# Moving one small weight transfer to the head of the load queue in a decode kernel

## The chip, the cores and the metric

The kernel runs on one core of one Trainium2 chip. The metric is device time in microseconds (us) of the whole kernel; the median of several runs is compared.

## What is computed

Two blocks share one normalised input, and their results are added to the input. Block A is attention of one new token per batch row over a cache of 4096 keys and values (4 batch rows, 32 heads, head width 128); block B is a gated MLP with a layer norm on one half of its hidden vector. All inputs are bf16.

```python
xn = layernorm(x)                                   # x: (4, 1, 640)
q  = (xn @ wq) as (B, H, 1, 128)                    # wq: (640, 4096)
p  = softmax(q . k_cache * 128**-0.5)               # k_cache: (4, 32, 4096, 128)
A  = (p . v_cache) @ wo                             # v_cache alike, wo: (4096, 640)
z  = gelu(xn @ w_in)                                # w_in: (640, 1728)
z1, z2 = z[..., :864], layernorm(z[..., 864:])
B  = (z1 * (w_sp * z2 + b_sp)) @ w_out              # w_out: (864, 640)
return x + A + B
```

The two caches are 268 MB of the 282 MB that the kernel reads.

## The kernel before

**Stages.** The kernel first normalises x, computes q for all heads (L287) and block B (L309 to L367), and then streams the caches in units of one batch row and eight heads, 8 MB each: 16 units of K and 16 of V. A K unit is transposed by DVE in eight pieces (L389), each followed by matmuls that give scores (L400). After four K units of one group of heads comes the softmax of that group (L407 to L465), and the four V units follow (L474), interleaved with K units of the next group. At the end the attention output is multiplied with wo (L517), added up (L565 to L580) and stored in two halves (L583).

**Buffers.** One buffer `kv` of five slots holds everything that is loaded in bulk: first the weights wq (slots 0 and 1), w_in and the first 512 rows of w_out (slot 2), then the cache units and wo. A unit takes two half slots or slots, and may be loaded once the work on what lay there is done.

**The remaining 352 rows of w_out.** They do not fill 128 partitions and are loaded by four transfers into two tiles `w_rest` (L128), which are taken from the pool of the transposed keys, `kT`. The table `RB` gives each transfer's partition block, first column, number of groups and columns:

```python
RB = ((0, 0, 8, 7), (0, 7, 5, 1), (1, 0, 3, 7), (1, 7, 3, 2))
```

The first of them moves 224 rows, 280 KB, in 32 pieces of 8,960 B; the others move 25, 105 and 30 KB. The first and third go to one tile, the second and fourth to the other, which GpSimd zeroes before (L123). In the trace the four transfers are carried by eight, five, three and three of the 16 DMA engines (so many increments of their semaphores follow each); the loads of 128 partitions by all 16.

**The queue.** All large loads are issued by SyncE (SP), one after another. An issue that has to wait for a buffer or a semaphore holds up the issues behind it. Before, SP issues in this order:

1. wq (L111), w_in (L114), w_out's first 512 rows (L118)
2. the four w_rest transfers (L128)
3. the K units 0, 1, 2, ... and V units (L167), with parts of wo among and behind them (L175)
4. one half of the output (L583)

ScalarE (ACT) issues three tiny loads at the start (w_sp, b_sp and x; L105 to L108) and the other half of the output. In the trace each DMA engine works through SP's loads in the order of issue, and the engines run apart by up to 4 us; a load has landed once every engine that takes part in it has incremented the load's semaphore. The program uses eight semaphores, which go round among the loads.

Of the kernel before, what the change touches and what calls it, by code (L numbers as in the profile page):

```python
# [16 lines left out]
def kernel(  # L17
# [19 lines left out]
    nc = tc.nc  # L37
    P = 128
    B, Sq, D = A_x.shape
    _, H, Sk, Dh = A_k_cache.shape  # L40
    assert Sq == 1 and B == 4 and Dh == P and D % P == 0
    DC = D // P
# [12 lines left out]
    F2 = B_w_in.shape[1]  # L55
    Fh = F2 // 2
    FA = 4
    FR = 9
    RB = ((0, 0, 8, 7), (0, 7, 5, 1), (1, 0, 3, 7), (1, 7, 3, 2))
# [3 lines left out]
    NOUT = A_wo.shape[1]  # L63
# [27 lines left out]
    def at_slot(i, n, off=0):  # L91
        return kv[:, i * SL + off:i * SL + off + n]
# [6 lines left out]
    n_q = DC * H * Dh  # L99
# [7 lines left out]
    nc.scalar.dma_start(out=sb_bf[:, 0:1], in_=B_w_sp)  # L107
    nc.scalar.dma_start(out=sb_bf[:, 1:2], in_=B_b_sp[None, :])  # L108

    wq = at_slot(0, n_q).rearrange("p (c n) -> p c n", c=DC)  # L110
    nc.sync.dma_start(out=wq, in_=A_wq.rearrange("(p c) n -> p c n", c=DC))  # L111
    n_in = DC * F2
    w_in = at_slot(2, n_in).rearrange("p (c f) -> p c f", c=DC)
    nc.sync.dma_start(out=w_in, in_=B_w_in.rearrange("(p c) f -> p c f", c=DC))  # L114

    nf = FA * P
    w_out = at_slot(2, FA * NOUT, n_in).rearrange("p (c n) -> p c n", c=FA)
    nc.sync.dma_start(out=w_out, in_=B_w_out[0:nf, :].rearrange("(p c) n -> p c n", p=P))  # L118
    w_rest = []
    for k, n in ((0, 7), (1, 2)):  # L120
        t = ktpool.tile([P, NKT], F32, tag="kT", name=f"w_rest{k}")[:NRP].bitcast(BF16)[:, 0:n * NOUT]
        w_rest.append(t.rearrange("p (c n) -> p c n", c=n))
    nc.gpsimd.memset(w_rest[1].rearrange("p c n -> p (c n)").bitcast(F32), 0.0)  # L123
    r_at = [nf]
    for q, c0, ni, n in RB:
        r_at.append(r_at[-1] + 4 * ni * n)
        k = c0 // 7
        nc.sync.dma_start(out=w_rest[k][32 * q:32 * q + 4 * ni, 0:n].rearrange("p c n -> p (c n)"),  # L128
                          in_=B_w_out[r_at[-2]:r_at[-1], :].rearrange("(r i c) n -> i r (c n)", r=4, c=n))

    NB = 32 * FC
    z_at = n_in + FA * NOUT
# [19 lines left out]
    def unit(item, t0, t1):  # L152

        s0, s1 = place[item]
        assert s1 == s0 + 1 or t1 <= T // 2 or t0 >= T // 2
        if t0 >= T // 2:
            return at_slot(s1, (t1 - t0) * Dh, t0 * Dh - SL)
        return at_slot(s0, (t1 - t0) * Dh, t0 * Dh)

    def load_unit(item):  # L160
        key, u = item
        g, b = divmod(u, B)
        cache = A_k_cache if key == "k" else A_v_cache
        src = cache[b, g * HG:(g + 1) * HG].rearrange("e (m t) d -> (e m) (t d)", t=T)
        c = cuts.get(item, (0, T))
        for t0, t1 in zip(c[:-1], c[1:]):
            nc.sync.dma_start(out=unit(item, t0, t1), in_=src[:, t0 * Dh:t1 * Dh])  # L167


    wo_q = A_wo.rearrange("(g p c) n -> g p c n", p=P, c=HG)  # L170
# [2 lines left out]
    def load_wo(g, c_cuts=(0, HG)):  # L173
        for c0, c1 in zip(c_cuts[:-1], c_cuts[1:]):
            nc.sync.dma_start(out=wo_t[g][:, c0:c1, :], in_=wo_q[g][:, c0:c1, :])  # L175

    load_unit(seq[0])


# [70 lines left out]
    for q in range(4):  # L250
        nc.gpsimd.tensor_copy(out=SelE[32 * q:32 * q + 32, :, q % 2, :],
                              in_=b8[32 * q:32 * q + 32, 8:8 + HP, None].to_broadcast((32, HP, P // HG)))
# [10 lines left out]
                          in_=ident_f[:].rearrange("p (q x c) -> p q x c", q=2, c=C2))  # L263
# [55 lines left out]
    for (q, c0, ni, n), f0, f1 in zip(RB, r_at[:-1], r_at[1:]):  # L319
        f0, f1 = f0 - r_at[2 * q], f1 - r_at[2 * q]  # L320
        for a in range(2):
            nc.scalar.activation(out=zT[32 * q:32 * q + 32, a, FA + c0:FA + c0 + n, 0:4 * ni].rearrange("p c (i r) -> p c i r", r=4),
                                 in_=zr_ps[32 * q:32 * q + 32, a, f0:f1].rearrange("p (r i c) -> p c i r", r=4, c=n),
# [8 lines left out]
    z1, z2, t1 = z_f[:, 0, :], z_f[:, 1, :], z_f[:, 2, :]  # L332
# [28 lines left out]
    for f0 in range(0, FC, 4):  # L361
        for hf in range(NH):
            for fc in range(f0, min(f0 + 4, FC)):
                n = P if fc < FA else NRP
# [162 lines left out]
    for i, item in enumerate(seq):  # L527
        if i + 1 < len(seq):
            key, u = seq[i + 1]
            load_unit(seq[i + 1])  # L530
            if key == "k" and u == 2 * B - 1:
                load_wo(u // B - 1)
        else:
            load_wo(NG - 3)
            load_wo(NG - 2)
            load_wo(NG - 1, (0, 4, 6, 7, 8))
        key, u = item
        g, b = divmod(u, B)
        if key == "k":
            done = b == B - 1 and g > 0  # L540
            for k in range(8):
                emit_K(u, k)
                if done and k == 1:
                    emit_sel(g - 1)
                if done and k == 2:
                    emit_oT(g - 1)
                if done and k == 5 and g == 1:
                    emit_proj(g - 1)
            if b == B - 1:
                if g < NG - 1:  # L550
                    fill_qz(g + 1)
                softmax(g)
        else:
            emit_V(u)
# [6 lines left out]
    for c, hf in ((0, 0), (1, 0), (0, 1), (1, 1), (2, 0), (2, 1)):  # L561
        p = min(c, 1)
# [49 lines left out]
```

## Time and profile before

| | before |
|---|---|
| median of 3 runs (lowest to highest) | 663.13 us (663.09 to 663.36) |
| profiled execution, first to last instruction (span) | 661.2 us |
| moved by DMA | 282.58 MB, mean 427 GB/s |
| PE busy | 287.5 us (43% of the span) |
| DVE busy | 372.2 us (56%) |
| ACT, POOL busy | 73.6 us, 67.0 us |
| granted TensorE clock, mean | 0.728 |

The profiled execution is one execution; its span leaves out what lies ahead of the first and behind the last instruction, and it was 1.9 us shorter than the median of the runs. Times in views of the trace count from the start of the span. "SPq" is SyncE's own queue of issues; the duration of an issue there is the time in which SyncE is occupied with it, not the time of the transfer. In a table of stages each row gives the stretch, its length, for each engine the busy time and the number of instructions, the granted PE clock, the mean busy share of the 16 DMA engines and GB/s.

### The profile page before, as it was taken

What the parts mean: (1) busy time and instruction counts of PE and PEld (TensorE: products, weight loads), DVE (VectorE), ACT (ScalarE), POOL (GpSimd) and SP (SyncE); (2) the same over time, 40 slices, a digit from 0 to 9 for tenths busy, and PEclk for the clock granted to TensorE, in tenths of its full rate; (3) what the DMA queues carried; (4) which work ended last, traced back from release to release, by engine and by line L of the source; (5) the groups of instructions that cost most, each with busy time, mean ns of one, the idle gap of its engine ahead of it and who ended that gap; (6) DMA issues with size and microseconds to landing.
All of it is one profiled execution on the core that took longest, in us unless ns stands there. A gap on an engine that the chain in (4) does not pass through costs nothing.

```text
span 661.2 us, 5415 instructions
## 1 busy us (share of the span) xinstructions
PE 287.5 (43%) x2247; PEld 106.6 (16%) x2247; DVE 372.2 (56%) x306; ACT 73.6 (11%) x145; POOL 67.0 (10%) x137
## 2 busy tenths in 40 slices
PE   0436656446062555235436065533706244551236
PEld 0211212112011121111112022110202112120113
DVE  2229999766191759718356286764629175971112
ACT  0300000341100000430200000070110000043200
POOL 3600000031200000130300000030110000003300
PEclk9857788669577587676758577875858769766678
DMA  9999999999999999999999999999999999999996
GB/s 372 452 446 420 420 447 438 429 444 417 436 436 433 428 425 437 433 436 445 416 432 433 432 421 450 427 432 429 437 440 433 424 433 416 445 444 429 419 420 285
DMA packets 6930, 282.58 MB, mean 427 GB/s; under 512 B 811, under 2 KB 1091, under 8 KB 1487
## 3 DMA queue, kind: packets, MB, share of 16 engines
q1 hardware_dynamic: 6879, 282.24, 99.0%
q8 instruction: 17, 0.28, 0.2%
q14 instruction: 6, 0.05, 0.0%
q10 hardware_dynamic: 28, 0.01, 0.0%
HBM read 282.24 MB, written 0.01 MB: 427 GB/s over the span
## 4 chain that ended last, share of the span: by engine, by line
DMA 77%; DVE 9%; issue 8%; PE 4%; ACT 0%; SPq 0%; DVEq 0%; ACTq 0%
DMA kv<-in_A_k_cache_dram 46%; DMA kv<-in_A_v_cache_dram 26%; DVE kT L389 8%; PE O L474 4%; DMA kv<-in_A_wo_dram 4%; DMA kv<-in_A_wq_dram 2%; DVE pT_t L456 0%; ACT Zb L437 0%; DVE m L407 0%; ACT p_bf L450 0%; PE S L400 0%; PE misc L411 0%; SPq L128 0%; PE proj L517 0%; DVE o_q L569 0%
## 5 line engine op out<-in xcount | busy, mean ns | idle before, releaser
L389 DVE STREAM_TRANSPOSE kT<-kv 128x2048 f32<-128x2048 f32 x128 | 282.8, 2275 | 128.1 <-DMA kv<-in_A_k_cache_dram 128.1
L400 PE MATMUL S<-kT,QZ 128*32 128x512 bf16 x1024 | 187.1, 498 | 261.9 <-DVE kT L389 261.9
L400 PEld LDWEIGHTS <-QZ 128*32 128x32 bf16 x1024 | 59.8, 110 | 387.5 <-issue 323.2
L474 PE MATMUL O<-kv,Zb 128*32 128x512 bf16 x1024 | 75.0, 458 | 56.4 <-DMA kv<-in_A_v_cache_dram 49.5
L437 ACT ACTIVATE Zb<-pT_t,MkE 32x128 bf16<-32x128 bf16 x120 | 60.8, 507 | 117.6 <-PE O L474 104.6
L483 DVE TENSOR_TENSOR om<-O,Mk 128x512 f32<-128x512 f32 x15 | 10.4, 692 | 93.8 <-PE O L474 93.8
L435 POOL TENSOR_SCALAR Zb<-pT_t,MkE 32x128 bf16<-32x128 bf16 x60 | 43.1, 718 | 138.6 <-PE O L474 126.1
L474 PEld LDWEIGHTS <-Zb 128*32 128x32 bf16 x1024 | 34.0, 113 | 97.3 <-issue 69.6
L450 ACT ACTIVATE p_bf<-S,negmax 128x1024 bf16<-128x1024 f32 x4 | 4.5, 1115 | 403.7 <-DVE negmax L417 403.7
L433 DVE TENSOR_SCALAR Zb<-pT_t,MkE 32x128 bf16<-32x128 bf16 x76 | 25.1, 330 | 2.3
L375 POOL COPY QZ<-qT 32x32 bf16<-32x32 bf16 x16 | 5.0, 315 | 188.9 <-PE S L400 188.4
L484 DVE TENSOR_REDUCE R<-om 128x128 f32<-128x512 f32 x15 | 15.3, 1021 | 0.5
L456 DVE STREAM_TRANSPOSE pT_t<-p_bf 128x1024 bf16<-128x1024 bf16 (+1 forms) x8 | 9.6, 1240 | 5.5 <-ACT p_bf L450 5.5
L461 POOL TENSOR_SCALAR rs<-MkB,rowsum 128x4 f32<-128x4 f32 x4 | 1.2, 299 | 112.7 <-ACT p_bf L450 112.7
L507 POOL MEMSET oT<- 128x66 bf16 x4 | 0.5, 146 | 96.6 <-PE proj L517 96.6
L407 DVE TENSOR_REDUCE m<-S 128x1 f32<-128x1024 f32 x4 | 4.9, 1224 | 6.0 <-PE S L400 6.0
L486 DVE TENSOR_SCALAR R<-O,Mk 128x128 f32<-128x128 f32 x1 | 0.3, 350 | 14.0 <-PE O L474 14.0
L496 PE MATMUL misc<-R,SelX 128*128 128x512 f32 x8 | 4.5, 644 | 7.2 <-DVE R L484 5.5
L287 PE MATMUL q<-kv,xnT 128*32 128x512 bf16 x40 | 4.3, 614 | 6.4 <-DVE xnT L208 6.4
L463 PE MATMUL misc<-rs,SelE 128*128 128x4 f32 x8 | 2.4, 365 | 10.4 <-POOL rs L461 10.4
L191 DVE CAST kv<-kv 8x640 f32<-8x640 bf16 x1 | 0.5, 482 | 10.7 <-DMA kv<-in_A_x_dram 10.7
L499 DVE TENSOR_TENSOR om<-misc,h 128x512 f32<-128x512 f32 x4 | 2.8, 692 | 4.9 <-PE misc L496 4.9
(102 smaller groups left out, 80.0 us busy)
## 6 DMA issues: line engine op xcount, KB each, us to landing
kv<-in_A_k_cache_dram SPq DMA_DIRECT2D x8, 4096.0 KB, 30.5
kv<-in_A_v_cache_dram SPq DMA_DIRECT2D x1, 6144.0 KB
kv<-in_A_wq_dram SPq DMA_DIRECT2D x1, 5120.0 KB
kv<-in_A_wo_dram SPq DMA_DIRECT2D x3, 1280.0 KB
kv<-in_B_w_in_dram SPq DMA_DIRECT2D x1, 2160.0 KB, 19.8
kv<-in_A_v_cache_dram SPq DMA_DIRECT2D x1, 2048.0 KB
kv<-in_B_w_out_dram SPq DMA_DIRECT2D x1, 640.0 KB, 20.9
kv<-in_A_wo_dram SPq DMA_DIRECT2D x1, 640.0 KB
```

The lines of the kernel that those rows point to most:

```text
L375: nc.gpsimd.tensor_copy(out=QZ[r0:r0 + 32, :, :, :, 8 + 8 * hp], in_=qT[32 * g:32 * g + 32, NE * hp:NE * hp + NE].rearrange("p e a b -> p ...
L389: nc.vector.transpose(kT[:].rearrange("p (t r) -> p t r", r=32), kw)
L400: nc.tensor.matmul(S_ps[32 * q:32 * q + 32, i], lhsT=QZ[:, b, 2 * kh + w, e, w0:w0 + 32], rhs=kb[:, i, :, e, :, w], start=(b == 0 and k < ...
L407: nc.vector.tensor_reduce(out=m1[:], in_=S_ps[:].rearrange("p i t m -> p (i t m)"), axis=AX.X, op=ALU.max)
L433: nc.vector.tensor_scalar(out=dst, in0=src, scalar1=mk, scalar2=None, op0=ALU.mult)
L435: nc.gpsimd.tensor_scalar(out=dst, in0=src, scalar1=mk, scalar2=None, op0=ALU.mult)
L437: nc.scalar.activation(out=dst, in_=src, func=ACT.Copy, scale=mk)
L450: nc.scalar.activation(out=p_bf[:, M:M + NP], in_=S_ps[:].rearrange("p i t m -> p (i t m)"), func=ACT.Exp, bias=negmax[:, 0:1], scale=scal ...
L456: nc.vector.transpose(pT_t[:, j0:j1, :], blocks)
L474: nc.tensor.matmul(O_ps[32 * q:32 * q + 32, :, :], lhsT=Zb[b % 2][:, w].rearrange("p h c -> p (h c)"), rhs=vv[:, w * 4 * Dh:(w + 1) * 4 * ...
L483: nc.vector.tensor_tensor(out=om4[:], in0=O_ps[:], in1=Mk4[:, :, None].to_broadcast((P, 4, Dh)), op=ALU.mult)
L484: nc.vector.tensor_reduce(out=R, in_=om4[:].rearrange("p c d -> p d c"), axis=AX.X, op=ALU.add)
```

## The change

The first of the four w_rest transfers (224 rows, 280 KB, on eight DMA engines) is issued ahead of wq. The other three stay behind w_out. Scheduling-only dependencies (`after`) hold the loads of SP's queue in the order in which they are written; they add no wait on the chip. The tiles of `w_rest` are allocated, and the second is zeroed, at an earlier place of the source text. On ScalarE, VectorE, GpSimd and TensorE the built program has the same instructions in the same order as before.

```diff
-    wq = at_slot(0, n_q).rearrange("p (c n) -> p c n", c=DC)
-    nc.sync.dma_start(out=wq, in_=A_wq.rearrange("(p c) n -> p c n", c=DC))
-    ...
-    nc.sync.dma_start(out=w_in, in_=B_w_in.rearrange("(p c) f -> p c f", c=DC))
-    ...
-    nc.sync.dma_start(out=w_out, in_=B_w_out[0:nf, :].rearrange("(p c) n -> p c n", p=P))
...
-        nc.sync.dma_start(out=w_rest[k][32 * q:32 * q + 4 * ni, 0:n].rearrange("p c n -> p (c n)"),
-                          in_=B_w_out[r_at[-2]:r_at[-1], :].rearrange("(r i c) n -> i r (c n)", r=4, c=n))
+
+    def load_rest(j):
+        q, c0, ni, n = RB[j]
+        return nc.sync.dma_start(out=w_rest[c0 // 7][32 * q:32 * q + 4 * ni, 0:n].rearrange("p c n -> p (c n)"),
+                                 in_=B_w_out[r_at[j]:r_at[j + 1], :].rearrange("(r i c) n -> i r (c n)", r=4, c=n))
+
+    queue = [load_rest(0)]
+
+    def after(load):
+        tc.add_manual_dep(load.ins, queue[-1].ins.name,
+                          mybir.DependencyInfo(mybir.DependencyClass.NoSync, mybir.DependencyReason.SCHED_ONLY),
+                          reason="order on the queue")
+        queue.append(load)
+
+    ...
+    after(nc.sync.dma_start(out=wq, in_=A_wq.rearrange("(p c) n -> p c n", c=DC)))
+    ...
+    after(nc.sync.dma_start(out=w_in, in_=B_w_in.rearrange("(p c) f -> p c f", c=DC)))
+    ...
+    after(nc.sync.dma_start(out=w_out, in_=B_w_out[0:nf, :].rearrange("(p c) n -> p c n", p=P)))
+    for j in (1, 2, 3):
+        after(load_rest(j))
...
-            nc.sync.dma_start(out=unit(item, t0, t1), in_=src[:, t0 * Dh:t1 * Dh])
+            after(nc.sync.dma_start(out=unit(item, t0, t1), in_=src[:, t0 * Dh:t1 * Dh]))
```

More of the change, by code (lines that the diff above doesn't have):

```diff
@@ L108 @@
     nc.scalar.dma_start(out=sb_bf[:, 1:2], in_=B_b_sp[None, :])
-    wq = at_slot(0, n_q).rearrange("p (c n) -> p c n", c=DC)
[L111 to L118, printed above, removed]
     w_rest = []
@@ L123 @@
     nc.gpsimd.memset(w_rest[1].rearrange("p c n -> p (c n)").bitcast(F32), 0.0)
-    r_at = [nf]
+    r_at = [FA * P]
     for q, c0, ni, n in RB:
         r_at.append(r_at[-1] + 4 * ni * n)
-        k = c0 // 7
-        nc.sync.dma_start(out=w_rest[k][32 * q:32 * q + 4 * ni, 0:n].rearrange("p c n -> p (c n)"),
-                          in_=B_w_out[r_at[-2]:r_at[-1], :].rearrange("(r i c) n -> i r (c n)", r=4, c=n))
+    def load_rest(j):
[8 more added lines that the diff above has]
+        queue.append(load)
+    wq = at_slot(0, n_q).rearrange("p (c n) -> p c n", c=DC)
+    after(nc.sync.dma_start(out=wq, in_=A_wq.rearrange("(p c) n -> p c n", c=DC)))
+    n_in = DC * F2
+    w_in = at_slot(2, n_in).rearrange("p (c f) -> p c f", c=DC)
+    after(nc.sync.dma_start(out=w_in, in_=B_w_in.rearrange("(p c) f -> p c f", c=DC)))
+    nf = FA * P
+    w_out = at_slot(2, FA * NOUT, n_in).rearrange("p (c n) -> p c n", c=FA)
+    after(nc.sync.dma_start(out=w_out, in_=B_w_out[0:nf, :].rearrange("(p c) n -> p c n", p=P)))
+    for j in (1, 2, 3):
+        after(load_rest(j))
     NB = 32 * FC
```

## The prediction

> **What bounds the kernel now.** I began with the page: which engine is busy all the time, and what the DMA queues carry.
>
> ```profile
> DMA  9999999999999999999999999999999999999996
> ...
> q1 hardware_dynamic: 6879, 282.24, 99.0%
> q8 instruction: 17, 0.28, 0.2%
> q14 instruction: 6, 0.05, 0.0%
> ```
>
> The DMA engines are at 9 tenths or more in 39 of 40 slices, while PE is at 43% of the span and DVE at 56%. The loads of queue q1 fill 99.0% of 16 engines' span; instructions travel on the same engines (q8, q14). The chain of waits puts 77% on DMA, but names a new waiter at every step, so I asked the stages whether the queues ever run dry.
>
> ```profile
> 1.50:2.00 0.50, 0.00 (x0) 0.00 (x0) 0.00 (x0) 0.00 (x0) 0.50 (x2) 1.00 3.67 1065
> ...
> 16.00:24.00 8.00, 6.26 (x70) 2.91 (x70) 2.88 (x7) 0.59 (x1) 7.38 (x30) 1.00 1.14 486
> ...
> 25.00:41.00 16.00, 4.75 (x29) 2.14 (x29) 2.42 (x7) 4.93 (x14) 5.86 (x10) 0.61 1.02 440
> ```
>
> ```profile
> 655.00:656.00 1.00, 0.99 (x16) 0.70 (x16) 0.26 (x2) 0.00 (x0) 0.00 (x0) 1.00 0.77 303
> 656.00:657.00 1.00, 0.70 (x12) 0.40 (x10) 0.00 (x0) 0.00 (x0) 0.00 (x0) 1.00 0.53 200
> 657.00:658.00 1.00, 1.00 (x19) 0.61 (x14) 0.66 (x2) 0.00 (x0) 0.00 (x0) 1.00 0.19 69
> ```
>
> The last two columns are the DMA share and GB/s (a packet counts where it starts, hence 3.67). No stage after the start is short of work. At the end the share falls 0.77, 0.53, 0.19: the 16 engines do not finish together, and the output waits for the last. So I need the 16 finishing times. The trace holds each engine's increment of a load's semaphore; worked out from these records, behind the first engine (us):
>
> ```
> k0, first at 41.00:      .01 .04 .11 .14 .17 .85 1.32 1.38 1.43 1.49 1.50 1.59 3.24 3.42 4.06
> last wo, first 653.96:   .63 1.17 1.77 2.74 2.75 2.77 2.85 2.90 3.09 3.61 3.77 4.10 4.10 4.16 4.17
> ```
>
> Behind the first row stand the four w_rest transfers. They increment 8, 5, 3 and 3 engines, so with 280, 25, 105 and 30 KB three engines carry 35 + 5 + 35 + 10 = 85 KB more, two carry 40, three carry 35, eight nothing ("the upper eight"; the others "the lower eight"). A 40,960 B packet takes 1.514 us, so 85 KB are 3.22 us, 40 are 1.51 and 35 are 1.32: the steps of that row. One upper engine also started 0.7 late (wq lands on 15 engines by 15.16, on it at 15.84: the .85).
>
> The second row has other steps because of q8: each of its 17 packets sets one engine back by about 1.5 us, and they go round eight engines. Following the increments from load to load, the first, ninth and seventeenth (40.6, 350.0, 647.6 us) hit the same engine, by the counts an upper one: 3 x 1.5 = 4.5, less a drift of the first engine itself of about 0.2. Two lower engines with 35 KB extra are hit twice, 1.32 + 2 x 1.5 = 4.3, and a third lower one is set back by q14. These are the last four, 4.10 to 4.17: one upper, three lower. That the one is upper is inferred, not shown by a row.
>
> **The start, step by step.**
>
> ```profile
> 0.71 0.39 SPq L111 DMA_DIRECT2D kv<-in_A_wq_dram  x1
> 1.17 0.41 SPq L114 DMA_DIRECT2D kv<-in_B_w_in_dram  x1
> 1.62 0.46 SPq L118 DMA_DIRECT2D kv<-in_B_w_out_dram  x1
> 2.12 0.88 SPq L128 DMA_DIRECT2D w_rest<-in_B_w_out_dram  x1
> ```
>
> *Removed and added on SP:* one issue of 0.88 us, the first of L128, moves from behind w_out to the head. wq's issue starts at 0.71 + 0.88 + 0.05 (the gap from 3.00 to the next issue, 3.05) = 1.64 instead of 0.71. Its first packets came at 1.73, 1.02 after their issue began, so on the upper eight, which have nothing of w_rest, they come at 2.66: **+0.93**. The bounds: 0.44, if at the head it costs what the 16-engine issues cost (0.39 and a gap), to 0.93, its own row. I take 0.93, the same instruction.
>
> *Lower eight:* w_rest's first packets come 1.02 after issue, at 1.73, or up to 0.49 later if data wait for the longer issue (0.88 against 0.39). Four packets of 338 ns are 1.35 us, to 3.1 at least, and wq is there at 2.66: no hole. The first wq packet of each engine took 2.0 to 2.8 us, not 1.51, a start-up loss of 0.5 to 1.3; on a first packet of 8,960 B it may be smaller or larger by some 0.5, which no row shows. Bounds -0.5 to +1.0; I take **+0.1**, near the low end: the tiny w_sp load on ACT's queue, which also goes to fewer than 16 engines, was issued at 0.71 too, for 0.53 us, and its packet started at 1.61, 0.90 after its issue began, no later than wq's.
>
> The row for all this is that each engine goes on to its next load by itself: k0 lands on an upper engine at 41.00 and on a lower one at 45.06. [...]
>
> *Taken away behind w_out:* nothing. Each engine moves the same bytes, in another order.
>
> *Waits.* Eight semaphores go round among the loads. Before, the fourth w_rest transfer shared wq's and waited for it:
>
> ```profile
> SPq L128 <- DMA kv<-in_A_wq_dram: 11.2, 1, 11.2
> ...
> SPq L167 <- POOL qT L298: 7.9, 1, 7.9
> ```
>
> By the built programs, after the change it shares one of the tiny loads on ACT's queue, and k0 shares that of the moved transfer, landed by about 5 us. Behind k0's issue on SP stand all later loads. It moves from 16.62 to about 8, and that is worth nothing: w_in, w_out and w_rest keep the engines busy until 21.2, when the first k0 packet starts. k1 still waits for POOL's qT, at 25.05, 16 us before the first engine is through k0.
>
> *Hidden:* wq lands at 15.84 + 0.93 = 16.8 on the upper engines, or 15.16 + 1.32 + at most 0.5 = 17.0 on the lower; the q matmuls began at 17.74, for xnT. x shares four lower engines with the moved transfer and may land earlier or later than 10.66; qT could be 16 us late before an engine starves, and after that it costs us for us. The w_rest matmuls (36.5 to 39.2) end before k0 lands (45.06). DVE, ACT, POOL and PE keep their instruction order.
>
> **Sum.** Upper: 4.10 to 4.17, +0.93; lower: 4.17 + 0.1. The last finish moves from 4.17 to 5.03 or 5.10, by **+0.87**, and the closing matmuls, L580 and the stores move with it. The profiled span is 661.2 us, the median 663.13: 1.9 lie outside, untouched. Span 662.1, median **664.0**. A measurement of this kernel can tell about 0.2%, 1.33 us, so this counts as no change.
>
> **Rivals.**
> - *The late start is free* (663.1; from 662.9 to 663.4). If the seventeenth q8 packet meets a lower engine, or the head issue costs the upper eight little, then the upper engines end at most at 3.09 + 0.93 = 4.02, before the lower ones' 4.17. For it: most of the 85 KB imbalance is still there as slack; against it: the counts of 8, 5 and 3 fit only with an upper engine among the last four. Chance 0.22.
> - *Slower by more than 0.2%* (664.8). The late starter: the 0.7 us that one upper engine lost at the first wq packet (15.84 against 15.16) may meet the deciding engine, now that the two halves start apart. 0.93 + 0.7 = +1.6. It decides once the start-up loss of that engine grows by over 0.46 (1.33 less 0.87). For it: first packets differ by 0.8 us; against: it is one engine in 16. Chance 0.16.
> - *Faster by more than 0.2%* (661.6). It needs 1.4 us off the last engine. Perfect balance of the second row gives that (mean 2.8 of 4.2), but the move shifts no byte between engines; smaller first packets give at most 0.5, to the lower half only. Chance 0.03.
> - *The order is not changed on the chip*, because a scheduler reorders: the built program has the moved issue at the head, so only 0.01.
>
> **Numbers.** Forecast case (+0.4 to +1.3) 0.58, and the cases above. Faster 0.04, same 0.79, slower 0.17: the slower rival and a little of the forecast's upper end. The range for 8 in 10 reaches from the free late start, 662.9, to the late starter, 664.8.
>
> **What would show it.** SP's timeline: moved issue at 0.71, wq's at about 1.64. Windows: the DMA share after the start lower until about 2.7. wq's landing between 16.5 and 17.3; k0's issue before 10 us; the L128 wait for wq gone. At the end one upper engine alone about 0.9 behind the rest, a last window 658:659 with a little DMA, o_bf at 659.4 instead of 658.57. Wrong: a hole in the DMA share later than 5 us, the q8 packets meeting other engines (the trace's increments show both), or a time outside 662.9 to 664.8.

## The result and the profile after

The changed kernel takes 665.26 us (median of 17 runs, 664.77 to 666.46). The kernel before takes 663.29 beside it (17 runs, 663.09 to 666.0). The ratio is 1.0023 [1.0015, 1.0031], a loss of about 1.5 us or 0.2%. The medians lie 2.0 apart; the ratio is smaller because some runs of the kernel before lie well above its median. The profiled execution of the changed kernel took 664.77 (span 663.0), the lowest of its runs. The forecast was 664.0 in a range of 662.9 to 664.8, so the time lies outside it, above.

The page of the changed kernel, DMA by slices and the queues (packets, MB, share of 16 engines' span):

```profile
DMA  8999999999999999999999999999999999999996
...
q1 hardware_dynamic: 6879, 282.24, 98.7%
q8 instruction: 17, 0.28, 0.2%
q14 instruction: 6, 0.05, 0.0%
```

The same packets and bytes, with the first slice thinner. The kernel is as DMA-bound as before. SP's timeline of the changed kernel (start, time that the issue occupies SP):

```profile
0.72 0.89 SPq L121 DMA_DIRECT2D w_rest<-in_B_w_out_dram  x1
1.66 0.46 SPq L133 DMA_DIRECT2D kv<-in_A_wq_dram  x1
2.17 0.42 SPq L136 DMA_DIRECT2D kv<-in_B_w_in_dram  x1
2.63 0.43 SPq L140 DMA_DIRECT2D kv<-in_B_w_out_dram  x1
3.10 2.41 SPq L121 DMA_DIRECT2D w_rest<-in_B_w_out_dram  x3
5.56 18.38 SPq L180 DMA_DIRECT2D kv<-in_A_k_cache_dram  x2
```

The issues stand where the prediction put them: wq at 1.66 (forecast 1.64). The last row joins k0's issue, at 5.56 instead of 16.62, and k1's, at 23.60 instead of 25.05. What SP waits for in the first 60 us:

```profile
SPq L180 <- DMA kv<-in_A_wq_dram: 10.9, 1, 10.9
...
SPq L180 <- POOL qT L311: 6.7, 1, 6.7
```

The wait for wq has moved from the fourth w_rest transfer to k1, and behind it POOL's qT still decides k1. The stages of the changed kernel, start and middle (the last two columns are DMA share and GB/s):

```profile
1.50:2.00 0.50, 0.00 (x0) 0.00 (x0) 0.00 (x0) 0.00 (x0) 0.50 (x2) 1.00 0.00 0
2.00:4.00 2.00, 0.00 (x0) 0.10 (x1) 0.00 (x0) 1.28 (x1) 0.91 (x6) 1.00 0.90 307
16.00:24.00 8.00, 5.56 (x69) 3.04 (x70) 2.15 (x3) 0.58 (x1) 6.68 (x28) 1.00 1.12 476
25.00:41.00 16.00, 4.75 (x29) 2.13 (x29) 2.42 (x7) 5.19 (x14) 4.59 (x6) 0.55 1.06 457
```

No load of SP's queue has a packet before 2.0, where the kernel before had a share of 3.67 in 1.5:2.0. w_rest's first packet comes at 2.40, 1.68 after its issue began, and the upper eight engines get their first packet of wq at 3.51; the forecast was 1.73 and 2.66. Later stages show no hole. wq lands at 16.40 to 16.86 (before 14.88 to 15.84). The end of the changed kernel, and the last addition from its timeline:

```profile
655.00:656.00 1.00, 0.71 (x12) 0.36 (x7) 0.97 (x2) 0.00 (x0) 0.00 (x0) 1.00 0.83 341
656.00:657.00 1.00, 0.25 (x4) 0.19 (x5) 0.57 (x2) 0.00 (x0) 0.00 (x0) 1.00 0.73 289
657.00:658.00 1.00, 1.00 (x16) 0.57 (x11) 0.00 (x0) 0.00 (x0) 0.00 (x0) 1.00 0.64 239
658.00:659.00 1.00, 0.69 (x11) 0.52 (x10) 0.00 (x0) 0.00 (x0) 0.00 (x0) 1.00 0.12 45
659.00:660.00 1.00, 0.91 (x19) 0.53 (x15) 0.89 (x3) 0.00 (x0) 0.00 (x0) 1.00 0.03 10
```

```profile
660.33 0.32 DVE L593 TENSOR_TENSOR o_bf<-last,o_q 64x160 bf16<-64x160 f32 x1
```

A share of 0.12 in 658:659 is about two of 16 engines, and 0.03 in 659:660 is half a microsecond of one engine: that is the lone engine. The finishing times, from the engines' increments of the semaphores as in the prediction (us behind the first engine):

```
k0, first at 42.48:      .10 .19 .23 .27 .37 .38 .38 .44 .51 .60 .62 1.64 2.19 2.30 3.10
last wo, first 655.47:   .12 .16 .92 1.84 2.71 2.74 2.76 2.77 2.98 2.99 3.05 3.20 3.20 3.38 4.41
```

The first row began at 41.00 before: the upper engines are 1.48 later at k0, while the last, a lower one, went from 45.06 to 45.58, by 0.52. In the second row one engine ends 1.03 behind all others, at 659.88, 1.75 later than the last one before (658.13). The next ends at 658.85. The run's time follows the last landing: 664.77 - 659.88 = 4.89, before 663.13 - 658.13 = 5.00, and between 4.85 and 5.00 in every profiled run below.

So the picture is the forecast's, but the step at the start is 1.5 us and not 0.93.

### The profile page after: what moved, and what is told of

Same layout as the page of the kernel before. It is cut to its first block, busy times and chain, and to the rows that moved or that the text cites. A ratio compares the mean times of both kernels' runs of the same rounds, so it can differ in the third digit from the quotient of the medians.

```text
span 663.0 us, 5416 instructions
## 1 busy us (share of the span) xinstructions
PE 280.9 (42%) x2247; PEld 105.5 (16%) x2247; DVE 372.2 (56%) x306; ACT 73.7 (11%) x145; POOL 66.9 (10%) x137
## 4 chain that ended last, share of the span: by engine, by line
DMA 74%; DVE 12%; issue 11%; PE 2%; SPq 1%; ACT 0%; DVEq 0%; ACTq 0%
DMA kv<-in_A_k_cache_dram 65%; DVE kT L402 11%; DMA kv<-in_A_v_cache_dram 5%; DMA kv<-in_A_wo_dram 4%; PE O L487 1%; SPq L121 0%; DVE pT_t L469 0%; PE S L413 0%; DVE Zb L446 0%; DVE m L420 0%; ACT p_bf L463 0%; PE proj L530 0%; DVE o_q L582 0%; PE misc L424 0%; DVE o L578 0%
## 5 line engine op out<-in xcount | busy, mean ns | idle before, releaser
L413 PE MATMUL S<-kT,QZ 128*32 128x512 bf16 x1024 | 184.0, 491 | 265.4 <-DVE kT L402 265.4
L487 PE MATMUL O<-kv,Zb 128*32 128x512 bf16 x1024 | 71.6, 441 | 60.1 <-DMA kv<-in_A_v_cache_dram 49.3
L530 PE MATMUL proj<-kv,oT 128*8 128x320 bf16 x54 | 5.6, 350 | 1.3 <-DMA kv<-in_A_wo_dram 1.3
```

The lines of the kernel that those rows point to most:

```text
L413: nc.tensor.matmul(S_ps[32 * q:32 * q + 32, i], lhsT=QZ[:, b, 2 * kh + w, e, w0:w0 + 32], rhs=kb[:, i, :, e, :, w], start=(b == 0 and k < ...
L487: nc.tensor.matmul(O_ps[32 * q:32 * q + 32, :, :], lhsT=Zb[b % 2][:, w].rearrange("p h c -> p (h c)"), rhs=vv[:, w * 4 * Dh:(w + 1) * 4 * ...
L530: nc.tensor.matmul(dst[0:nb, 0:n1 - n0], lhsT=state[("oT", g)][:, c0:c0 + nb], rhs=wo_t[g][:, c, n0:n1], start=start, stop=stop)
```

## The experiments

The questions: is the loss in the late start of the upper engines at all, or in the early k0 issue and the new semaphores, or in having any other load ahead of wq; and why is that start 0.55 later than the moved issue explains? The theories' letters are those of the expectations. Medians of the kernel before beside the runs were 663.3 to 663.4. Edits are against the changed kernel unless said. In e1, e2, e6, e9, e10 and e12 the 95% interval of the ratio includes 1, because the runs of the kernel before scatter upward (663.03 to 666.1 beside e10). Where a version differs by less than 1 us, its lowest run says more: 664.17 in e9 and 663.98 in e10, with 663.16 and 663.03 for the kernel before beside them.

First a table of the runs that change what stands at the head of the queue, then each run by itself. The packets and landings are those of the one profiled execution of each, the median is that of all its runs. The head of the changed kernel was profiled a second time, in e6: wq's first packet came at 3.48 and k0 landed first at 42.92, against 3.51 and 42.48. So the table does not resolve differences of under some 0.4 us between landings.

| run | load ahead of wq (on eight engines unless said) | first packet of wq | first landing of k0 | last landing of wo | median |
|---|---|---|---|---|---|
| before | none | 1.73 | 41.00 | 658.13 | 663.3 |
| e1_behind_wq | none | 1.72 | 40.94 | 658.33 | 663.48 |
| e2_wout_head | 640 KB on all 16 | 3.56 | 40.75 | 658.46 | 663.43 |
| e10_small_head | 40 KB | 2.74 | 41.94 | 659.33 | 664.18 |
| e14_half_head | 160 KB | 2.85 | 42.17 | 659.65 | 664.46 |
| after | 280 KB | 3.51 | 42.48 | 659.88 | 665.26 |
| e3_third_head | 105 KB on three engines | 2.72 | 42.24 | 659.68 | 664.59 |
| e4_two_heads | 280 KB, and 105 KB on three | 3.84 | 43.35 | 661.82 | 666.77 |
| e9_wide_first | 280 KB on all 16 | 2.75 | 42.13 | 659.61 | 664.26 |

**e1_behind_wq: the narrow transfer second, behind wq.**

```diff
-    queue = [load_rest(0)]
+    queue = [nc.sync.dma_start(out=wq, in_=A_wq.rearrange("(p c) n -> p c n", c=DC))]
...
+    after(load_rest(0))                     # ahead of w_in
```

> The moved transfer stands second, behind wq and ahead of w_in; all else, the semaphores that the loads share included, is as in the changed kernel. Theory A (the narrow transfer at the head makes the upper eight engines start late, and one of them is the last to finish): the upper eight start at 1.7 us again, time 663.3 (663.0 to 663.6). Theory B (the other waits on SP's queue and k0's early issue cost the time): 665.2, as changed.

663.48, ratio 1.0002 [0.999, 1.0013]. SP's timeline of this run:

```profile
0.72 0.39 SPq L125 DMA_DIRECT2D kv<-in_A_wq_dram  x1
1.16 0.86 SPq L121 DMA_DIRECT2D w_rest<-in_B_w_out_dram  x1
```

One place further back, the same issue of 0.86 us and the same 280 KB cost nothing: wq's first packets start between 1.72 and 2.83 (before, 1.73 to 2.15), and every engine has work while SP issues. It is the head of the queue that costs. On the early k0 issue this run says nothing, against what its expectation took for granted: the fourth w_rest transfer again shared wq's semaphore and was issued at 16.11, k0 at 16.89.

**e2_wout_head: a wide load at the head instead, all four narrow ones behind w_in.**

```diff
-    queue = [load_rest(0)]
+    queue = [nc.sync.dma_start(out=w_out, in_=B_w_out[0:nf, :].rearrange("(p c) n -> p c n", p=P))]
...
-    for j in (1, 2, 3):
+    for j in (0, 1, 2, 3):
```

> At the head stands w_out's first part (640 KB), which goes over all 16 engines; the four w_rest transfers stand behind w_in. Theory A: all engines get their first packet at about 1.7 us, no engine loses anything, 663.3. Theory C (whatever is put ahead of wq costs, since wq and q come later): by the issue of 0.46 us alone 663.8, by wq landing 1.6 us later up to 664.9.

663.43, ratio 1.0004 [0.9995, 1.0012]. SP's timeline of this run:

```profile
0.72 0.39 SPq L127 DMA_DIRECT2D kv<-in_B_w_out_dram  x1
1.16 0.41 SPq L136 DMA_DIRECT2D kv<-in_A_wq_dram  x1
...
5.45 0.41 SPq L180 DMA_DIRECT2D kv<-in_A_k_cache_dram  x1
```

640 KB over 16 engines stand ahead of wq, their first packet comes at 1.73, k0 is issued at 5.45, and k1 still waits for wq and then for qT. No loss. That rejects theory C (any load ahead of wq) and theory B (the early k0 issue and the shifted semaphores), which this run has as the changed kernel has it.

**e3_third_head: the third narrow transfer at the head (105 KB, three engines).**

```diff
-    queue = [load_rest(0)]
+    queue = [load_rest(2)]
...
-    for j in (1, 2, 3):
+    for j in (0, 1, 3):
```

> At the head stands the third w_rest transfer (105 KB, three engines) instead of the first (280 KB, eight engines). Theory A: what counts is the narrow issue ahead of wq, not its bytes, so 13 engines start late by the same 1.5 us and the time is that of the changed kernel, 665.2 (664.8 to 665.6). Theory D (the bytes at the head set the delay): 105/280 of it, 664.0.

664.59, ratio 1.0012 [1.0002, 1.0021]. It lies between the 665.2 of A and the 664.0 of D. The issue took 0.91 us, the first k0 landing came 1.24 later than before. A narrow head costs this much on three engines too, so it is not the count of eight.

**e4_two_heads: the first and the third ahead of wq.**

```diff
     queue = [load_rest(0)]
+    after(load_rest(2))                     # ahead of wq
...
-    for j in (1, 2, 3):
+    for j in (1, 3):
```

> The first and the third w_rest transfer both stand ahead of wq: two narrow issues. Theory A: each delays the upper eight, a second one by at least its issue of 0.75 to 0.88 us, so 666.1 to 666.8, and the upper engines land k0 2.3 to 3.0 us later than before instead of 1.5. Rival E (the loss is paid once, at the start of the queue, whatever stands there): 665.2.

666.77 (five runs), ratio 1.0043 [1.003, 1.0056], in A's range (666.1 to 666.8). SP's timeline, with wq behind two heads:

```profile
0.71 1.71 SPq L121 DMA_DIRECT2D w_rest<-in_B_w_out_dram  x2
2.47 0.60 SPq L134 DMA_DIRECT2D kv<-in_A_wq_dram  x1
```

wq's issue is now 1.75 late, the first k0 landing 2.35, the last wo landing 3.69 (661.82 against 658.13). A second narrow head takes the loss from 2.0 to 3.4 us, so it is not paid once, and rival E falls. But the engine that ends last is another one here. By the increments, the one that the seventeenth instruction packet hits ends at 660.79, 2.66 later than the last one before, near the 2.35 at k0. The last one, at 661.82, is hit by the fourth and the twelfth packet and was already 2.8 behind the first engine at k0. So the time fits A's range partly by luck, and the way from the late start to the last landing rests on the next two runs.

**e6_after_fewer_pe and e7_before_fewer_pe: fewer instructions, so one instruction packet less.** The same edit in both kernels, the changed one (e6) and the one before (e7), leaves out 28 of the 64 value matmuls in each of six V units:

```diff
+            if 1 <= v <= 6 and 4 <= w < 60 and w // 4 % 2:
+                continue
```

> The changed kernel, with 28 of the 64 value matmuls left out in each of the second to seventh V units (336 TensorE instructions fewer; the loads and all else as they are), so that at least one of the 17 instruction packets is not fetched. Theory A (the deciding engine is an upper one that started late and is hit by three instruction packets): without the third its finish falls from 4.4 us behind the first engine to about 2.9, the next ones at 3.4 decide, and the time falls by 0.7 to 1.0 us to 664.2 to 664.6. Theory F (all engines, or the compute at the end, are late alike): it stays at 665.2.

> The kernel before, with the same 336 TensorE instructions left out. Theory A: four engines finish within 0.07 us of each other and only one of them loses its third instruction packet, so the time stays at 663.2 to 663.4. Theory F: no change either; the gap to the run without these instructions of the changed kernel stays at 1.9, where theory A has it at about 1.0.

e6: 663.76, ratio 0.9995 [0.9986, 1.0004]; e7: 663.22, ratio 0.9989 [0.998, 0.9998]. Queue q8 has 16 packets instead of 17. The end of e6:

```profile
658.00:659.00 1.00, 0.91 (x17) 0.48 (x16) 0.82 (x3) 0.00 (x0) 0.00 (x0) 1.00 0.22 81
659.00:660.00 1.00, 0.30 (x4) 0.08 (x3) 0.61 (x2) 0.00 (x0) 0.00 (x0) 1.00 0.00 0
```

The lone engine is gone: the last two landings are 658.95 and 658.94, and no DMA is left in 659:660. The changed kernel falls by 1.5 us, more than the expected 0.7 to 1.0, and the gap between the two kernels shrinks from 2.0 us to 0.54. Most of the loss is therefore carried by the one engine that the seventeenth packet hits, as the forecast had inferred from counts. That the fall is larger than expected fits the later start of this execution (k0 first at 42.92, not 42.48): with a third packet its upper engine would have stood further behind the rest than 1.03. In the kernel before the same edit moved the median by 0.1 to 0.2, but its runs now lie within 663.12 to 663.54, where those of the whole kernel reach 665.8.

**e8_act_later: ACT's tiny loads later.**

```diff
+    held = const.tile([P, 1], F32)
+    nc.gpsimd.memset(held[:], 1.0)
+    hold = nc.scalar.activation(out=held[:], in_=held[:], func=ACT.Sqrt)
...
-    nc.scalar.dma_start(out=sb_bf[:, 0:1], in_=B_w_sp)
+    behind(nc.scalar.dma_start(out=sb_bf[:, 0:1], in_=B_w_sp))   # the other two alike
```

> The changed kernel, but ACT first runs one small activation, so that its three tiny loads are issued at about 3.3 us instead of 0.7 to 2.2, after SP's first four loads. Theory G (the narrow transfer and wq come late because ACT's loads are described at the same time, by a part that both queues share): the narrow transfer's first packet at 1.73 instead of 2.40, wq's first on the upper engines at 2.7 to 2.9 instead of 3.51, time 664.4 to 664.7. Theory H (the narrow transfer itself takes this long to be described, by its rows): first packets stay at 2.40 and 3.51, time 665.2.

665.1, ratio 1.0019 [1.0009, 1.0029]: no gain. The tiny loads were issued at 1.41 to 2.45, earlier than the expected 3.3 but no longer first. The narrow transfer's first packet came at 2.33, not at G's 1.73. wq's first packet came at 3.10 instead of 3.51, yet on the upper engines those packets took 2.4 to 2.9 us instead of 1.7 to 2.1, and the first k0 landing was at 42.87. Theory G, that ACT's loads beside the narrow one hold it up, is rejected for the time. It is also a warning: the start of a first packet alone does not price a start.

**e9_wide_first: the same 224 rows at the head, dealt to 16 engines.** The rows are laid to partitions in another order, and the reading of the products is changed to match.

```diff
-                                 in_=B_w_out[r_at[j]:r_at[j + 1], :].rearrange("(r i c) n -> i r (c n)", r=4, c=n))
+        src = B_w_out[r_at[j]:r_at[j + 1], :]
+        src = src.rearrange("(p c) n -> p (c n)", c=n) if j == 0 else src.rearrange("(r i c) n -> i r (c n)", r=4, c=n)
```

> The moved transfer stays at the head with its 280 KB in 32 rows, but the 224 rows of w_out are dealt out so that its outer dimension is 32 and all 16 engines carry two rows each (block B's gelu writes its values in the same new order, so the result is the reference's). Theory A with H: a wide issue costs 0.4 us, its first packet comes at 1.73 and wq's follow without a gap, so nobody starts late; each upper engine has 17.5 KB more (0.65 us), each lower one as much less, and the upper one with three instruction packets decides: 663.9 to 664.1. Theory I (any small load ahead of wq costs what was measured): 665.2.

664.26, ratio 1.0006 [0.9997, 1.0016], a little above the expected 663.9 to 664.1. SP's timeline of this run:

```profile
0.72 0.39 SPq L123 DMA_DIRECT2D w_rest<-in_B_w_out_dram  x1
1.16 0.41 SPq L134 DMA_DIRECT2D kv<-in_A_wq_dram  x1
```

The issue costs 0.39 instead of 0.89 and the first packet comes at 1.74. That is 1.0 us better than the changed kernel, and theory I falls. It is not as good as before: 0.65 us were expected for the two more pieces on each upper engine, and these occupied an engine for 1.0 us (1.74 to wq's first packet at 2.75), with a median of 470 ns a piece instead of 338. How much of that is the start of the queue and how much the wide form is not separated here; the experiment after the next has the wide form away from the start.

**e10_small_head: the same rows and engines, but one column block of seven (40 KB) at the head.**

```diff
-    def load_rest(j):
+    def load_rest(j, a=0, b=None):          # columns a to b only
...
-    queue = [load_rest(0)]
+    queue = [load_rest(0, 0, 1)]
...
+    after(load_rest(0, 1, 7))               # behind w_out
```

> At the head stand the same 32 rows on eight engines, but only one of their seven columns (40 KB, 32 pieces of 1,280 B); the other six follow behind w_out as a transfer of their own. Theory H (a narrow transfer is described row by row, some 0.035 us each, and wq's description stands behind it): wq's first packet on the upper eight at 3.5 us as in the changed kernel, k0 there 1.5 us later than before, time 665.2 (664.8 to 665.5). Theory D (the bytes at the head set the delay, a seventh of them here): wq's first packet before 2.8, time 663.6.

664.18, ratio 1.0009 [0.9997, 1.0021], between the 663.6 of D and the 665.2 of H, both of which fall. The issue of this run and its start:

```profile
0.72 0.88 SPq L122 DMA_DIRECT2D w_rest<-in_B_w_out_dram  x1
```

```profile
2.00:4.00 2.00, 0.00 (x0) 0.10 (x1) 0.00 (x0) 1.28 (x1) 0.92 (x6) 1.00 1.22 348
```

With a seventh of the bytes the issue takes as long (0.88, against 0.89 with 280 KB), and in the 16-engine form of e9 it took 0.39: here the price of the issue is one of shape and not of size. wq starts at 2.74 and the first k0 landing is 0.94 late. The issue of wq moved by 0.95 and its first packet by 1.01, so this is the forecast's +0.93 nearly by itself.

**e11_wide_behind: the wide form of e9 in the place where the kernel before has the narrow one.** The mapping of e9, with wq first and `for j in (0, 1, 2, 3)` behind w_out.

```diff
-    queue = [load_rest(0)]
+    queue = [nc.sync.dma_start(out=wq, in_=A_wq.rearrange("(p c) n -> p c n", c=DC))]
...
-    for j in (1, 2, 3):
+    for j in (0, 1, 2, 3):
```

> The wide transfer (32 outer rows, all 16 engines, w_out's 224 rows dealt out anew) behind w_out instead of at the head. Theory A: wq starts at 1.73 as before; each upper engine still has 17.5 KB, 0.65 us, more than before, and the upper one with three instruction packets decides: 663.9 to 664.0. If the wide transfer at the head costs nothing beyond its bytes, this equals its time there, 664.26; what it is below that is the price of the head for a wide load.

665.14, ratio 1.0026 [1.0016, 1.0035], where 663.9 to 664.0 was expected: a miss. The stage in which these pieces run, in e11:

```profile
21.00:25.00 4.00, 3.78 (x46) 1.97 (x39) 1.85 (x2) 0.92 (x2) 3.01 (x13) 1.00 1.20 389
```

and the same stage in the kernel before:

```profile
21.00:25.00 4.00, 3.20 (x42) 1.77 (x35) 1.94 (x2) 1.49 (x2) 3.01 (x14) 1.00 1.26 539
```

The engines are as busy (1.20 against 1.26) and move 389 GB/s instead of 539. The 8,960 B pieces of the first and third transfer took a median of 464 ns (338 to 720) instead of 338, the 1,280 B pieces 106 instead of 55, and the 65,536 B packets beside them up to 3.7 us instead of 2.4. So where all 16 engines wrote into 32 partitions, these pieces and the packets beside them took longer than where eight engines did (464 ns against 338, up to 3.7 us against 2.4). Why they did is not shown by any run here. In the balance of bytes this version is better than both kernels, and it is still slower.

**e12_act_first: the narrow transfer first on ACT's queue, wq first on SP's.**

```diff
-        return nc.sync.dma_start(out=...
+        return (nc.scalar if j == 0 else nc.sync).dma_start(out=...
...
-    queue = [load_rest(0)]
+    queue = [nc.sync.dma_start(out=wq, in_=A_wq.rearrange("(p c) n -> p c n", c=DC))]
```

> The narrow transfer is the first load on ACT's queue instead of SP's; wq is again SP's first, both issued at 0.71. Theory J (each queue has its loads described by itself): wq's first packet at 1.73, k0 lands on the upper engines as before, 663.2 to 663.5. Theory K (one part describes the loads of both queues, one load after another): whichever is taken first, wq's first packets come between 2.4 and 3.5 and the time is 664.4 to 665.2, unless wq is taken first, when it is 663.3 and w_rest's first packet comes after wq's.

664.15 (663.5 to 665.62), ratio 1.0007 [0.9997, 1.0018]. ACT's timeline of this run:

```profile
0.72 1.29 ACTq L117 DMA_DIRECT2D w_rest<-in_B_w_out_dram  x1
```

ACT's three tiny loads stand behind it. The issue takes 1.29 us here, wq's first packet comes at 1.74, and w_rest's own first packet only at 5.38: wq was served first, so this is no second way to the head. It repairs most of the loss, but x, behind it on ACT's queue, lands at 16.4 to 18.4 instead of 10.6, and k1 is issued at 32.77. The first k0 landing is 0.23 late, the last wo landing 0.83. It meets neither expectation, and where its 0.8 comes from stays open.

**e14_half_head: four of the seven column blocks (160 KB) at the head.**

```diff
-    queue = [load_rest(0)]
+    queue = [load_rest(0, 0, 4)]
...
+    after(load_rest(0, 4, 7))               # behind w_out
```

> At the head stand four of the seven columns (160 KB in 32 pieces of 5,120 B, eight engines), the other three behind w_out. With one column wq's first packet on the upper eight came at 2.74 and the time was 664.18, with seven 3.51 and 665.26. Theory M (while the lower eight work on the bytes of the head, wq's description for the upper ones is held up, more for more bytes): wq's first packet between 2.8 and 3.4, k0 on the upper eight 1.1 to 1.4 us later than before, time 664.5 to 664.9. [...]

664.46, ratio 1.0011 [1.0002, 1.002], just under the 664.5 to 664.9 of theory M, by which the bytes on the lower eight hold up wq on the upper eight. With e10 and the changed kernel the first k0 landing is 0.94, 1.17 and 1.48 late for 40, 160 and 280 KB. The medians, 664.18, 664.46 and 665.26, go the same way. From 40 to 280 KB the step is 0.54 us in the changed kernel and 0.98 in e6, which has the same head and landed k0 first 1.92 late. Each of eight engines has 30 KB more for it, which take 1.16 us (30 / 35 of four pieces of 338 ns, 1.35): about half of this time or more reaches engines that carry none of it. That more at the head costs more is shown. Whether the bytes count or the size of the pieces is not: the 32 pieces grow with the bytes (1,280, 5,120, 8,960 B), and with a scatter of 0.4 this run does not tell the two apart. What passes the delay on is not shown either. It isn't ACT's loads (e8) and not the number of rows (e10).

## Why the prediction was wrong in size and right in kind

**The step that failed: the upper engines' late start.** The prediction sized it as the moved issue alone, "**+0.93**", and gave as its bounds 0.44 to 0.93: it took the larger end, but let nothing lie above. Measured, the upper engines are 1.48 late at k0. e10 confirms the 0.93 for the issue (0.94 with 40 KB), and the changed kernel shows the missing term, +0.54 for what the other engines carry at the head (+0.98 in e6). The wrong idea behind it was that an engine without bytes of the narrow transfer is not touched by it. The row quoted for that, the different landings of k0, shows engines that drift apart in a full stream, and says nothing of a start. An estimate that leaves eight engines idle for the narrow transfer's own time, four pieces of 338 ns or 1.35 us, would have been nearer to the 1.48 than my row, but by chance: with 40 KB, four pieces of some 55 ns on an engine, the same estimate gives 0.2, and e10 measured 0.94.

**Lower eight.** "+0.1" was taken of -0.5 to +1.0. w_rest's first packet came at 2.40, later than the 1.73 to 2.22 that the working allowed. Measured +0.5 at k0, and +0.7 at the end (658.85 against 658.13, the last that is not the lone one). Inside the bounds, and without weight: the upper one decides.

**The end.** The lone upper engine is there, 1.03 behind the rest (forecast about 0.9), and it is the one that is set back three times, at 39.8, 351.7 and 648.6, by the increments. That it is upper was inferred before; e6 shows now that it is the seventeenth packet that makes it the last. Its landing moved by 1.75, not 0.87. Of that 0.94 is the issue, 0.54 the load on the other engines, and about 0.25 came on the way to the end and is not explained. The rest of the distance, from the profiled 664.77 to the median 665.26, is how this execution lies among its runs: it is the fastest of 17. In e6 and e8, with the same narrow transfer at the head, k0 landed first 1.92 and 1.87 late, and wq's first packets on the upper engines took 2.0 to 2.5 and 2.4 to 2.9 us, not 1.7 to 2.1. So the usual run of the changed kernel probably starts later than the profiled one; that is not shown, as no second run of it was profiled.

**Costed at nothing, and worth nothing.** The early k0 issue and the other semaphores: e2 has them and stands at 663.43. wq landed at 16.40 to 16.86, inside the 16.5 to 17.3 but for its first engines, and what follows on it stayed hidden. x landed by 9.14 (10.62 before); which engines carried it no record shows. k1 waits for qT as forecast. The bytes behind w_out: e1 moves the same transfer without a loss.

**The rivals.** The free late start (663.1) is rejected by the lone engine at the end. "Slower by more than 0.2%" is the side that came, but not by its mechanism: it wanted one upper engine to lose another 0.7, whereas all of them lost about 0.55 in the profiled execution and more in e6. The chance of that side was too small because a load that starts an empty queue had no row in the trace, and the range's upper end was set by a rival rather than by that missing row. Neither a gain nor an unchanged order had any part in it.

**The signs named beforehand.** The issues at 0.72 and 1.66, the empty DMA share at the start, wq's landing, k0's early issue and the lone engine all came. o_bf came at 660.33 (forecast 659.4), and DMA reached into 659:660: those two were the sign that the size was off.

No version was faster than the kernel before. e1 and e2 are equal to it within their intervals; e7 leaves work out.

## What to carry to other kernels

In a kernel bound by DMA, look at what stands first on the load queue. In this one 640 KB over all 16 engines ahead of wq cost nothing that could be measured (663.43 against 663.4). A narrow load there cost 0.9 us by its issue, with 40 KB as with 280, and from 40 to 280 KB another 0.54 to 0.98 us, about half or more of the added transfer time of 1.16, on engines that had no part in it; one place further back it cost nothing that could be measured (663.48). The delay from the start was still there at the end: 1.48 us at k0's first landing and 1.75 at the last landing of wo, 617 us later. So look at the finishing time of each DMA engine, not at the mean share. And a start has to be priced by a row of a start: where the trace has none of that shape, the bound is open above.

## What was not expected of the hardware

- Instruction packets steered the end. By the increments each of the seventeen packets of q8 sets one engine back by about 1.5 us (the one at 614.0 in the kernel before: from 1.52 to 3.06 behind the first engine), and leaving out enough matmuls to save the last one took 1.5 us off the changed kernel and most of the scatter out of the other (663.12 to 663.54 instead of 663.16 to 665.82). Which engine a packet hits is read from the increments, not recorded.
- The issue of the narrow transfer takes 0.86 to 0.91 us for 40, 105 and 280 KB on SP, 1.29 on ACT's queue, and 0.39 in its 16-engine form. At the head of SP's queue its first packet comes 1.6 to 1.7 us after the issue began, that of a wide one 1.02.
- Where sixteen engines wrote 32 partitions (e11), the pieces of 8,960 B took a median of 464 ns; they took 338 where eight engines did so behind w_out (the kernel before).
